# One core, a gated linear attention feeding four experts: the first chunk loaded in rows of four tokens, with new plans for the transfers of the later chunks

## The chip, the cores and the metric

The kernel runs on one core of a Trainium2 chip. The metric is the device time of the program in microseconds (us), as the median of several executions. Each execution comes with the span of its instructions, the clock that TensorE was granted, and a state, fast or slow. A ratio is the mean time of one kernel's fast runs over that of the other's of the same rounds, so it isn't quite the ratio of the medians quoted.

Engines: PE is TensorE, PEld its weight load, DVE VectorE, ACT ScalarE, POOL GpSimd, SP SyncE. SPq and ACTq are the queues on which SyncE and ScalarE issue transfers.

## The reference

```python
B, H, S, D = 4, 8, 768, 48                     # q, k, v, f_logit
f = 1 / (1 + exp(-f_logit))
for t in range(S):
    state = f[:, :, t, :, None] * state + einsum('bhd,bhe->bhde', k[:, :, t], v[:, :, t])
    y[:, :, t] = einsum('bhd,bhde->bhe', q[:, :, t], state)
x = y as (3072, 384)
p = domain_probs / (domain_probs.sum(-1) + 1e-9)
out = sum over 4 experts of p[:, e] * (relu(x @ w1[e]) @ w2[e])     # w1 384x1024, w2 1024x384
```

## The kernel before

The sequence is cut into six chunks of 128 tokens. For each chunk and batch the kernel forms decays (two "gates", a cumulative sum on TensorE, exponentials), multiplies q and k by them, transposes both, multiplies them with each other ("at"), masks the product, multiplies it by v ("y"), and transposes the result into xT, the experts' input. Chunks 0 and 1 are transposed on TensorE, chunks 2 to 5 by a transfer (`dma_tp`).

All instructions are put in order before the program runs. A small planner in Python gives each operation a cost, a priority, its inputs and its buffers, walks through time, and writes the engines' instruction streams in the order that comes out. The hardware then runs each stream strictly in this order.

```python
class Plan:
    def run(self):
        ...
        for e in ("PE", "ACT", "DVE", "POOL", "DMA"):
            ...   # first operation, by priority, whose inputs and buffers are ready
            o.engine, o.start, o.end = e, now, now + o.costs[e]
...
rooms = {"ps_m": 4, "ps_t": 4, "f": 4, "q": 4, "k": 4, "v": 4, ...}     # f, q, k, v: half chunks
...
def load(c, nm, b, n):
    ins[c, nm, b] = nc.sync.dma_start(out=tl(nm, c, b // 2)[:, hh(b, n), :],
                                      in_=srcs[nm][c, :, b * H:(b + n) * H, :])
def dma_tp(c, b):
    nc.sync.dma_start_transpose(out=tl("QK", c, b)..., in_=tl("qk", c, b)...)
...
P.add(f"ld {nm}{c}.{b}", {"DMA": 1.05 * n}, ..., lag=2.0)               # n batches in one load
P.add(f"tp {c}.{b}", {"DMA": 1.8}, on(dma_tp), ..., lag=2.2)
P.add(f"at {c}.{b}", {"PE": 0.35}, on(pe_at), s(7), deps=[et])          # needs tp
P.add(f"store {c}.{nt}.{part}", {"DMA": 0.6}, ...)
...
o.pad, t = int((o.start - t) / 0.2), o.end      # filler matmuls up to the first expert matmul
```

## Time and profile before

| | value |
|---|---|
| time | 304.68 us (304.61 to 305.26, 3 runs) |
| span of the profiled run | 302.7 us |
| first expert matmul | 22.74 us |
| from there to the end ("body") | 280.0 us |
| mean granted clock of TensorE | 0.999 |

Two rows of the page's picture of 40 equal slices: the first is TensorE's busy tenths, the second the clock it was granted.

```profile
PE   7899999999999999999999999999999999999995
...
PEclk9999999999999999999999999999999999999999
```

The table by stretches, asked for the body alone, gives its length, then each engine's busy time (PE first), then granted clock, DMA share and GB/s. TensorE is idle for 280.0 - 274.6 = 5.4 us of the body.

```profile
22.74:302.70 279.96, 274.56 (x1913) 156.62 (x1944) 121.55 (x238) 155.65 (x265) 82.09 (x134) 1.00 0.59 114
```

### The profile page before, as it was taken

What the parts mean: (1) busy time and instruction counts of PE and PEld (TensorE: products, weight loads), DVE (VectorE), ACT (ScalarE), POOL (GpSimd) and SP (SyncE); (2) the same over time, 40 slices, a digit from 0 to 9 for tenths busy, and PEclk for the clock granted to TensorE, in tenths of its full rate; (3) what the DMA queues carried; (4) which work ended last, traced back from release to release, by engine and by line L of the source; (5) the groups of instructions that cost most, each with busy time, mean ns of one, the idle gap of its engine ahead of it and who ended that gap; (6) DMA issues with size and microseconds to landing.
All of it is one profiled execution on the core that took longest, in us unless ns stands there. A gap on an engine that the chain in (4) does not pass through costs nothing.

```text
span 302.7 us, 5517 instructions
## 1 busy us (share of the span) xinstructions
PE 293.2 (97%) x2112; PEld 169.4 (56%) x2143; DVE 138.1 (46%) x273; ACT 170.8 (56%) x295; POOL 95.5 (32%) x157
## 2 busy tenths in 40 slices
PE   7899999999999999999999999999999999999995
PEld 5565555567775655455555555555555555555553
DVE  6774013787853764516555344544423443201223
ACT  5767654857865444676356475345566344475440
POOL 4584400409656237423426143522332100000000
PEclk9999999999999999999999999999999999999999
DMA  7999999954994589866997877301322201100003
GB/s 157 203 193 204 207 206 193 228 83 91 217 207 84 111 161 187 189 122 120 182 187 134 216 142 147 56 13 28 100 61 51 48 14 30 67 22 2 0 0 106
DMA packets 137355, 36.10 MB, mean 119 GB/s; under 512 B 128496, under 2 KB 135792, under 8 KB 137328
## 3 DMA queue, kind: packets, MB, share of 16 engines
q1 hardware_dynamic: 131568, 29.45, 49.1%
q0 software_dynamic: 5760, 6.29, 12.4%
q8 instruction: 17, 0.28, 0.4%
q14 instruction: 10, 0.08, 0.1%
HBM read 31.51 MB, written 4.72 MB: 120 GB/s over the span
## 4 chain that ended last, share of the span: by engine, by line
PE 88%; DMA 4%; DVE 2%; SPq 2%; issue 1%; POOL 1%; ACT 1%; DVEq 0%; ACTq 0%; POOLq 0%
PE ps_m L356 41%; PE ps_m L344 40%; DMA w_sb<-in_moe_w_dram 3%; PE ps_t L300 2%; SPq L222 2%; DMA f<-in_f_logit_dram 1%; PE ps_t L315 1%; PE ps_t L321 1%; PE ps_t L311 1%; PE ps_t L255 1%; PE ps_t L285 1%; DVE qk L276 1%; POOL qk L276 0%; DVE AT L304 0%; POOL Sf L335 0%
## 5 line engine op out<-in xcount | busy, mean ns | idle before, releaser
L352 ACT ACTIVATE h<-ps_m 128x512 bf16<-128x512 f32 (+1 forms) x171 | 98.3, 577 | 103.0 <-PE ps_m L344 92.9
L356 PE MATMUL ps_m<-w_sb,h 128*128 128x384 bf16 x776 | 153.0, 324 | 0.2
L344 PE MATMUL ps_m<-xT,w_sb 128*128 128x512 bf16 (+1 forms) x593 | 150.4, 362 | 2.1 <-DVE o L367 0.3
L356 PEld LDWEIGHTS <-h 128*128 128x128 bf16 x776 | 73.0, 98 | 57.0
L363 DVE SCALAR_TENSOR_TENSOR o<-ps_m,pn,o 128x384 f32<-128x384 f32 (+1 forms) x73 | 44.6, 611 | 96.8 <-PE ps_m L356 89.4
L344 PEld LDWEIGHTS <-w_sb 128*128 128x128 bf16 x624 | 59.8, 98 | 47.1 <-issue 0.7
L276 POOL TENSOR_TENSOR qk<-q,e 128x384 bf16<-128x384 f32 x19 | 22.8, 1204 | 64.9 <-ACT e L262 64.4
L304 DVE TENSOR_TENSOR AT<-ps_t,mask 128x512 bf16<-128x512 f32 x48 | 31.1, 683 | 19.2 <-PE ps_t L300 19.1
L335 POOL TENSOR_TENSOR Sf<-Sf,egs 48x192 f32<-48x192 f32 x40 | 20.4, 510 | 48.8 <-DVE Sf L328 46.8
L350 DVE TENSOR_SCALAR h<-ps_m 128x512 bf16<-128x512 f32 (+1 forms) x37 | 20.7, 572 | 22.0 <-PE ps_m L344 19.8
L276 POOL TENSOR_TENSOR qk<-k,e 128x384 bf16<-128x384 f32 x20 | 21.0, 1052 | 19.8 <-ACT e L264 12.9
L262 ACT ACTIVATE e<-ps_t 128x384 f32<-128x384 f32 x24 | 20.7, 864 | 3.7 <-PE ps_t L255 2.4
L328 DVE TENSOR_TENSOR Sf<-Sf,ps_t 48x192 f32<-48x192 f32 x40 | 14.0, 349 | 6.1 <-PE ps_t L321 5.3
L336 POOL CAST sb<-Sf 48x192 bf16<-48x192 f32 x40 | 13.6, 339 | 2.6
L365 ACT ACTIVATE o<-ps_m,pn 128x384 f32<-128x384 f32 x20 | 11.6, 580 | 3.9 <-PE ps_m L356 3.1
L264 ACT ACTIVATE e<-ps_t 128x384 f32<-128x384 f32 x24 | 13.0, 541 | 0.0
L556 PE MATMUL ps_m<-busy 128*128 128x256 bf16 x71 | 11.5, 301 | 1.3 <-DVE busy L140 1.3
L218 DVE CAST yb<-ps_t 128x384 bf16<-128x384 f32 x16 | 8.9, 555 | 7.4 <-PE ps_t L315 6.3
L247 ACT ACTIVATE ex<-f 128x768 f32<-128x768 f32 (+1 forms) x14 | 10.5, 748 | 3.1 <-DMA f<-in_f_logit_dram 2.9
L315 PE MATMUL ps_t<-vb,AT 128*128 128x48 bf16 x192 | 11.4, 184 | 0.7 <-DVE vb L218 0.7
L315 PEld LDWEIGHTS <-AT 128*128 128x128 bf16 x192 | 9.8, 97 | 3.0 <-issue 1.0
L251 ACT ACTIVATE gp<-ex 128x768 bf16<-128x768 f32 (+1 forms) x14 | 10.5, 751 | 0.4
(50 smaller groups left out, 139.9 us busy)
## 6 DMA issues: line engine op xcount, KB each, us to landing
w_sb<-in_moe_w_dram POOLq DMA_DIRECT2D x8, 768.0 KB, 18.8
out_dram<-o SPq DMA_DIRECT2D x23, 192.0 KB, 2.1
f<-in_f_logit_dram SPq DMA_DIRECT2D x10, 384.0 KB, 4.3
k<-in_k_dram SPq DMA_DIRECT2D x10, 384.0 KB, 5.2
q<-in_q_dram SPq DMA_DIRECT2D x10, 384.0 KB, 5.3
v<-in_v_dram SPq DMA_DIRECT2D x10, 384.0 KB, 5.5
f<-in_f_logit_dram SPq DMA_DIRECT2D x4, 192.0 KB, 4.0
k<-in_k_dram SPq DMA_DIRECT2D x4, 192.0 KB, 4.0
```

The lines of the kernel that those rows point to most:

```text
L262: nc.scalar.activation(out=e[:, 0].rearrange("t (d h) -> t h d", d=D), in_=cs[:, 0:HD].rearrange("t (i r d) -> t r i d", r=2, d=D), func=A ...
L276: engines[eng].tensor_tensor(out=tl("qk", c, b)[:, j, :, 0:D].rearrange("t (i r) d -> t i r d", r=2), in0=tl("qk"[j], c, b // 2)[:, hh(b), ...
L304: nc.vector.tensor_tensor(out=tl("AT", c, b)[:, r].rearrange("s i t -> s (i t)"), in0=tl("A", c, b, r).rearrange("s i t -> s (i t)"), in1= ...
L315: nc.tensor.matmul(out=y[:, h * D:(h + 1) * D], lhsT=AT[:, r, i, :], rhs=vb[:, h, :], start=(c == 0), stop=True, skip_group_check=True)
L328: nc.vector.tensor_tensor(out=Sf[rows, b], in0=Sf[rows, b], in1=KV[rows, :, r, :], op=ALU.add)
L335: nc.gpsimd.tensor_tensor(out=Sf[rows, b], in0=Sf[rows, b], in1=eg, op=ALU.mult)
L336: nc.gpsimd.tensor_copy(out=nb[rows, b, :, r * D:(r + 1) * D], in_=Sf[rows, b])
L344: nc.tensor.matmul(out=tl("hp", c, e, fc, n0)[:, n0:n1], lhsT=w1_sb[:, e, kk, fc * 128:(fc + 1) * 128], rhs=tl("xT", c)[:, kk, n0:n1], sta ...
L350: nc.vector.tensor_relu(out=dst, in_=src)
L352: nc.scalar.activation(out=dst, in_=src, func=AF.Relu)
L356: nc.tensor.matmul(out=tl("op", c, e, nt, part)[:, cols], lhsT=tl("h", c, e)[:, fc, nt * T:(nt + 1) * T], rhs=w2_sb[:, e, fc, cols], start ...
L363: nc.vector.scalar_tensor_tensor(out=o, in0=op, scalar=pe, in1=o, op0=ALU.mult, op1=ALU.add)
```

## The change

The intent is an earlier start of the experts. The first chunk's tokens are dealt out so that a partition row holds four of them. f, q and k then come in packets of 768 B in place of 192 B. Gates and exponentials run over half of the heads for all batches at once; the price is a re-layout of k by 16 small transfers, a permuted mask, and 16 stores for the chunk in place of 4. One PSUM tile holds all eight banks. Alongside, the planning of the later chunks is redone: new costs of transfers, a model of the queue's run-ahead, buffers for whole chunks, exponentials in two planned steps.

```diff
-    LATENCY = 0.2
+    LATENCY, AHEAD = 0.2, 0.06
...
+    def by_tail(self, ops, shift):            # first chunk: priority by the longest way to its end
...
+                    if o.ring is not None:
+                        self.ring = max(self.ring, o.end) + o.ring
+                        o.end = max(o.end, self.ring - 4.0)
+                        o.lag = self.ring - o.end + 1.6
...
-    rooms = {..., "f": 4, "q": 4, "k": 4, "v": 4, ...
+    rooms = {..., "ps_c": 2, "ps_a": 4, "f": 2, "q": 2, "k": 2, "v": 2, ...
+    big = ps.tile([128, 8, 512], FP32, name="big")
...
+    def load0(nm, x, n):
+        if nm == "v":                          # block x: 32 partitions, 192 B runs
+            src = v.rearrange("b h (c p j) d -> c j p (b h) d", p=R, j=J)[0, x]
+            d = nc.sync.dma_start(out=tl("v", 0)[x * R:(x + 1) * R], in_=src)
+        else:                                  # 768 B runs of four tokens
+            src = a.rearrange("b h (c p j) d -> c b p h (j d)", p=R, j=J)[0, b, :, rows]
+            eng = nc.scalar if b % 2 and nm in "fk" else nc.sync
...
-            after(ins["w", 0], ins[0, "k", B - 1])
+            after(ins["w", 0], ins[0, "v", 0])
...
-        op = P.add(f"ld {nm}{c}.{b}", {"DMA": 1.05 * n}, ..., lag=2.0)
+        op = P.add(f"ld {nm}{c}.{b}", {"DMA": 0.6}, ..., ring=1.0 * n)
-        wd[i] = P.add(f"w {i}", {"DMA": 4.5}, ..., lag=2.0)
+        wd[i] = P.add(f"w {i}", {"W": 4.5}, ..., lag=1.5)
-                et = P.add(f"tp {c}.{b}", {"DMA": 1.8}, on(dma_tp), ..., lag=2.2)
+                et = P.add(f"tp {c}.{b}", {"DMA": 1.25}, on(dma_tp), ..., lag=2.9)
-                P.add(f"store {c}.{nt}.{part}", {"DMA": 0.6}, ...)
+                P.add(f"store {c}.{nt}.{part}", {"DMA": 0.45}, ..., ring=0.6)
...
+            for j in range(J):                 # store of the first chunk: four per tile
+                nc.sync.dma_start(out=rows[j], in_=tl("o", c, nt)[j * R:(j + 1) * R, :])
```

## The prediction

> **What bounds the kernel now.** I read the page first, and in it the shares of the engines:
>
> ```profile
> span 302.7 us, 5517 instructions
> PE 293.2 (97%) x2112; PEld 169.4 (56%) x2143; DVE 138.1 (46%) x273; ACT 170.8 (56%) x295; POOL 95.5 (32%) x157
> ```
>
> TensorE is busy for 97% of the span, but 11.5 us of this are 71 filler matmuls on the tile "busy", which only keep it occupied at the start. So two questions decide: when does its real work begin, and does it ever stop afterwards? The waits of TensorE from 23 us to the end answer the second. The columns are total us, times, longest:
>
> ```profile
> PE ps_m L344 <- DVE o L367: 0.3, 1, 0.3
> PE ps_t L285 <- DVE qk L276: 0.3, 1, 0.3
> PE ps_m L344 <- DMA w_sb<-in_moe_w_dram: 0.3, 1, 0.3
> ```
>
> That is the whole list: 0.9 us in 280 us. From the first expert matmul on the kernel is bound by TensorE; nothing that the other engines gain there counts. The timeline of the first 32 us gives that matmul and what ended just before it (start, us, engine, line, operation):
>
> ```profile
> 3.72 0.52 ACT L247 ACTIVATE ex<-f 128x384 f32<-128x384 f32 x1 [1.64 <-DMA f<-in_f_logit_dram]
> ...
> 10.20 1.28 DVE L304 TENSOR_TENSOR AT<-ps_t,mask 128x512 bf16<-128x512 f32 x2
> ...
> 14.63 6.77 POOL L229 DMA_DIRECT2D w_sb<-in_moe_w_dram  x8 [0.25 <-DMA k<-in_k_dram]
> ...
> 18.66 1.87 DVE L304 TENSOR_TENSOR AT<-ps_t,mask 128x512 bf16<-128x512 f32 x3
> ...
> 21.96 0.48 ACT L216 COPY xT<-ps_t 128x384 bf16<-128x384 bf16 x1 [0.73 <-PE ps_t L340]
> 22.74 0.98 PEld L344 LDWEIGHTS <-w_sb 128*128 128x128 bf16 x6 [0.55 <-DMA w_sb<-in_moe_w_dram]
> ```
>
> The first expert matmul starts at 22.74 us. Its input xT is complete at 21.96 + 0.48 = 22.44, its weights at about 22.7. **Two chains end within 0.3 us of each other**, and the change has to shorten both. The chain of waits, cut to 0 to 24 us, names the weights:
>
> ```profile
> 13.03 1.36 POOL qk L276
> 14.38 0.25 issue
> 14.63 8.07 DMA w_sb<-in_moe_w_dram
> ```
>
> The first weight request goes out at 14.63, once the last k has landed, and takes 8.07 us. The other chain is the first chunk's attention. Between 8.70 and 21.60 us the table by stretches has VectorE busy for 11.80 of 12.90 us (ScalarE 9.88): VectorE bounds it.
>
> **What the Trainium skill says.** "DMA: Bandwidth & Descriptors", section Specifications, puts the smallest transfer at line rate at 512 bytes. The trace agrees in direction: 128,496 of the 137,355 packets are under 512 B. In the trace's list of packets the median one of 192 B took 15 ns and one of 768 B 36 ns on its DMA engine; times 16 engines this is 205 and 341 GB/s. "ScalarE: Activation LUTs", What ACT_TABLE_LOAD costs, gives 186 ns + 0.833 ns per column with immediates, hence 506 for 384 columns and 826 for 768; the trace has 523 and 838. One pass of 768 thus saves about 0.2 us against two of 384. "SBUF — State Buffer", Who interferes with whom, says that a VectorE operation with two SBUF inputs blocks against a GpSimd one that reads SBUF. The trace agrees: GpSimd's k product takes 1.36 us in the start while VectorE multiplies, and VectorE's k product takes 0.54 alone there but 0.87 in the mean. So sharing products between them gains less than their count suggests.
>
> **The change, part by part.** Everything named here concerns the first chunk.
>
> *Loads.* f, q and k of the chunk are 3 x 0.786 = 2.36 MB. At 205 GB/s this is 11.5 us, at 341 GB/s 6.9: saved 4.6 us. v stays at 192 B (3.8 us). Traffic begins near 2.4 us, so k should be in SBUF at about 2.4 + 2 x 2.3 + 1 for completion = 8.0, q at 10.3, the first v at 2.4 + 6.9 + 1.0 + 1 = 11.3 and the last v at 14.2 (before: v was used up to 19.0).
>
> *First weights.* Their request now waits for the first v (11.3) in place of the last k (about 14.4). With the measured 8.07 us they arrive at 19.4, 3.3 us earlier. That is a floor for the start. The later ones arrived every 3.9 us of DMA (0.786 MB written at some 205 GB/s); TensorE uses two per 10.3 us (64 units of 0.65 us per chunk, 8 per weight), so no later weight should stop it.
>
> *ScalarE.* Before, four batches had 0.52 + 0.52 + 0.86 + 0.54 + 0.17 = 2.61 us each, 10.4 in all. Now 8 passes of 768 columns at 0.84: 6.7 us. It saves 3.7, but the first products move back: all four batches go through together. f's first half lands near 4.3; two gates to 5.9; two decay sums of 7 matmuls with 1536 columns (0.64 us each at the 0.216 us that 512 columns take) with waits to 7.5; the four exps to about 8.3, 9.0, 9.8 and 10.6. The first product starts at 8.4 instead of 6.42.
>
> *VectorE.* The eight masked copies stay at 0.67 us, 5.4 in all: still PSUM fp32, whatever the mask's type. The q product loses its strided e and should fall from 0.85 to about 0.55, like k's. I assume five of eight products on VectorE at 0.6 (3.0 us), three or four of the eight transposed copies at 0.38 (1.3), and few v and y copies, since ScalarE is free from 10.6. Sum 9.7 us, against 12.65 between 6.4 and 21.6 before. From 8.4, with 1 us lost waiting for q and for the first masked copy: 19.1.
>
> *The end of the chain.* From the last masked copy (18.66 + 1.87 = 20.53) to xT (22.44) were 1.9 us: y, its copy, transposes, their copy. The same four steps remain. 19.1 + 1.9 = 21.0; if more goes to ScalarE and GpSimd than I assume, 19.5. I take **20.5** as the start, against 22.74: 2.2 us.
>
> *Moved off the path.* The k tile is laid out again by 16 small transfers and the state sums wait for them; at some 0.5 us an issue they end near 24 us, and TensorE needs the last at about 26. Single PSUM tile, fewer pads, split exps of later chunks, other orders there: TensorE's work after the start is the same, so 0 us. The first chunk's stores become 4 issues each, near 80 us, where SyncE has slack.
>
> **Rivals.** *Weights bind alone:* if the attention is quicker than I think, the start stops at 19.4 (a gain of 3.3; 301.4 us). For it: the request still waits for 6.9 us of loads. *The attention is hardly quicker:* gathering all batches in one tile loses the overlap that batch 0 had (its first masked copy was at 10.20; now about 12.5). With VectorE then packed to 20 us the start is 22 and the time 304. For it: VectorE was the bound and its masked copies stay. *A new stall in TensorE's order:* state sums waiting for the k transfers behind the weight traffic, or the second chunk coming late because its requests are planned behind all weights; up to 2 us lost, 304 to 306. Against it: its first load still waits for the sixth weight, which itself comes earlier. *A wider gain,* over 6.1 us (2%), would need a start by 16.6, before the weights can be there: nearly excluded.
>
> **Range and chances.** 304.68 - 2.2 = 302.5; I lean slightly to the smaller side of the time, since the planner's priorities were redone for just this stretch: 302.3. Lower end 300.2: start at 18.3, weights a microsecond earlier than worked out. Upper end 304.5: the gain all but eaten by one of the two losing rivals. Both 2% lines (298.6 and 310.8) lie outside.
>
> **What would show it.** Right: packets of 192 B fewer by some 12,000; k used before 9 us; first weight request near 11.3; first masked copy near 12.5; the first expert matmul between 19.4 and 21.5; the difference of the times equal to the difference of these starts within 0.5 us; VectorE over 85% busy from 9 us to the last masked copy. Wrong: TensorE waits over 0.5 us after its start (third rival); the first expert matmul waiting for weights by over 1 us (first rival); or VectorE idle in the start, waiting for ScalarE or loads, which my sum does not contain.

## More of the kernel before

SyncE's queue near 70 to 93 us (start, us taken, line, operation, tensors, how many) shows the loads of chunk 2, the stores of chunk 0 and the first transposing transfers of chunk 2 sharing one queue:

```profile
71.23 0.59 SPq L222 DMA_DIRECT2D f<-in_f_logit_dram  x1
71.92 1.59 SPq L222 DMA_DIRECT2D k<-in_k_dram  x1
...
81.64 1.76 SPq L371 DMA_DIRECT2D out_dram<-o  x1
...
88.92 1.34 SPq L289 DMA_TRANSPOSE QK<-qk  x1
...
92.25 2.13 SPq L289 DMA_TRANSPOSE QK<-qk  x1
```

## The result and the profile after

| | before | after |
|---|---|---|
| time, median | 304.97 us (304.61 to 305.79, 4 runs) | 333.39 us (332.97 to 333.98, 4 runs) |
| span of the profiled run | 302.7 | 332.3 |
| first expert matmul | 22.74 | 27.47 |
| body | 280.0 | 304.8 |
| mean granted clock | 0.999 | 0.952 |

The ratio is 1.093 (1.090 to 1.096). The kernel became 28 us slower, far outside the range. Of the 29.6 us between the spans, **4.7 are a later start and 24.8 are in the body**, where the prediction had put zero.

The page's two rows show the body's loss. Three holes in TensorE's row (slices 12, 14 and 19 of 40) each stand beside a fall of the clock; a fourth fall, in slice 10, has no hole above it:

```profile
PE   5989999989959599995999999999999999999995
...
PEclk9959999995978989997899999999999999999999
```

The table by stretches, for the body of the changed kernel:

```profile
27.47:332.30 304.83, 287.30 (x1946) 160.96 (x1943) 122.13 (x239) 156.84 (x269) 80.37 (x132) 0.96 0.59 104
```

TensorE is idle for 304.8 - 287.3 = 17.5 us, 12.1 more than before. Its busy time grew by 12.7 us, although it does the same work after the start. The trace's clock records give four stretches of half clock in the body, 23.9 us in all, in which matmuls take about twice as long. TensorE was busy for 21.1 us of them; half of that, some 10.6 us, is most of the growth. The kernel before has none between 5.4 us and its last microsecond.

The list of TensorE's waits after the start (us in total, times, longest) names what it stood for. Like the body, it is read from one profiled execution of each kernel:

```profile
PE big L455 <- DMA QK<-qk: 7.8, 3, 3.8
PE big L413 <- ACT gp L329: 4.1, 2, 3.8
PE big L465 <- DVE AT L459: 0.5, 1, 0.5
```

L455 is "at", which waits for the transposed q and k (3.6 of the 7.8 us fall in chunk 2, the rest in chunk 3), and L413 the cumulative sum, which waits for the gates and so for f. SyncE's queue shows what is behind both:

```profile
69.80 8.55 SPq L530 DMA_DIRECT2D out_dram<-o  x16
...
80.27 0.51 SPq L283 DMA_DIRECT2D f<-in_f_logit_dram  x1
...
99.49 1.35 SPq L444 DMA_TRANSPOSE QK<-qk  x1
...
102.22 1.25 SPq L444 DMA_TRANSPOSE QK<-qk  x1
...
110.87 2.89 SPq L444 DMA_TRANSPOSE QK<-qk  x1
```

The 16 stores hold the queue for 8.55 us, f of chunk 2 is issued at 80.27 in place of 71.23, and the transposes at 99 to 115 in place of 89 to 105. It is tempting to stop here and blame the stores. The first experiment shows why that is not the cause.

The start, on ScalarE (start, us, what its idle time was waiting for):

```profile
5.94 0.84 ACT L332 ACTIVATE ex<-f 128x768 f32<-128x768 f32 x1 [3.85 <-DMA f<-in_f_logit_dram]
...
10.46 1.51 ACT L348 ACTIVATE e<-big 128x768 f32<-128x768 f32 x2 [1.12 <-PE big L344]
13.23 1.51 ACT L348 ACTIVATE e<-big 128x768 f32<-128x768 f32 x2 [1.26 <-PE big L344]
18.48 0.51 ACT L277 CAST vb<-v 128x384 bf16<-128x384 f32 x1 [3.73 <-DMA v<-in_v_dram]
18.90 1.55 ACT L277 COPY QK<-big 112x512 bf16<-112x512 bf16 x3
```

f arrives late, the decay sums take twice the predicted time (1.28 us; in s_warm below, with TensorE kept busy ahead of them, 0.66), and then ScalarE stands for v with three ready copies of q and k behind it.

### The profile page after: what moved, and what is told of

Read it like the earlier page. It is cut to its first block, busy times and chain, and to the rows that moved or that the text cites. A ratio compares the mean times of both kernels' runs of the same rounds, so it can differ in the third digit from the quotient of the medians.

```text
span 332.3 us, 5660 instructions
## 1 busy us (share of the span) xinstructions
PE 308.5 (93%) x2137; PEld 176.1 (53%) x2137; DVE 136.9 (41%) x268; ACT 170.6 (51%) x291; POOL 99.2 (30%) x165
## 4 chain that ended last, share of the span: by engine, by line
PE 74%; DMA 13%; issue 3%; SPq 3%; DVE 2%; ACT 2%; POOL 1%; ACTq 0%; POOLq 0%; DVEq 0%
PE big L510 34%; PE big L498 33%; DMA QK<-qk 4%; DMA f<-in_f_logit_dram 3%; DMA qk<-h 3%; PE big L455 2%; DMA v<-in_v_dram 2%; SPq L409 1%; SPq L283 1%; PE big L341 1%; DMA xT<-yb 1%; PE big L413 1%; PE big L469 1%; PE big L465 1%; PE big L475 1%
## 5 line engine op out<-in xcount | busy, mean ns | idle before, releaser
L498 PE MATMUL big<-xT,w_sb 128*128 128x512 bf16 (+1 forms) x624 | 158.6, 372 | 0.0
L506 ACT ACTIVATE h<-big 128x512 bf16<-128x512 f32 (+1 forms) x167 | 96.0, 578 | 117.5 <-PE big L498 107.9
L510 PE MATMUL big<-w_sb,h 128*128 128x384 bf16 x776 | 156.3, 329 | 0.0
L517 DVE SCALAR_TENSOR_TENSOR o<-big,pn,o 128x384 f32<-128x384 f32 (+1 forms) x73 | 44.6, 612 | 104.0 <-PE big L510 86.1
L504 DVE TENSOR_SCALAR h<-big 128x512 bf16<-128x512 f32 (+1 forms) x41 | 23.5, 580 | 33.4 <-PE big L498 33.1
L459 DVE TENSOR_TENSOR AT<-big,mask 128x512 bf16<-128x512 f32 x40 | 25.9, 685 | 22.7 <-PE big L455 22.6
L418 ACT ACTIVATE e<-big 128x384 f32<-128x384 f32 x20 | 17.3, 865 | 2.1 <-PE big L413 2.0
L482 DVE TENSOR_TENSOR Sf<-Sf,big 48x192 f32<-48x192 f32 x40 | 14.0, 350 | 9.5 <-PE big L475 8.7
L519 ACT ACTIVATE o<-big,pn 128x384 f32<-128x384 f32 x23 | 13.3, 580 | 5.4 <-PE big L510 4.7
L455 PE MATMUL big<-QK 48*128 48x128 bf16 x160 | 8.4, 227 | 8.0 <-DMA QK<-qk 7.8
L455 PEld LDWEIGHTS <-QK 48*128 48x128 bf16 x160 | 4.7, 97 | 15.4 <-DMA QK<-qk 9.7
L421 ACT ACTIVATE e<-big 128x384 f32<-128x384 f32 x20 | 10.9, 543 | 0.0
L465 PE MATMUL big<-sb,QK 112*128 112x96 bf16 x80 | 10.2, 206 | 0.6 <-DVE AT L459 0.5
L469 PE MATMUL big<-vb,AT 128*128 128x48 bf16 x160 | 10.4, 187 | 0.4 <-DVE AT L459 0.4
```

The lines of the kernel that those rows point to most:

```text
L418: nc.scalar.activation(out=e[:, 0].rearrange("t (d h) -> t h d", d=D), in_=cs[:, 0:HD].rearrange("t (i r d) -> t r i d", r=2, d=D), func=A ...
L455: nc.tensor.matmul(out=tl("A", c, b, r)[:, i, :], lhsT=QK[rows, 1, i, :], rhs=QK[rows, 0, i, :], start=True, stop=True)
L459: nc.vector.tensor_tensor(out=tl("AT", c, b)[:, r].rearrange("s i t -> s (i t)"), in0=tl("A", c, b, r).rearrange("s i t -> s (i t)"), in1= ...
L469: nc.tensor.matmul(out=y[:, h * D:(h + 1) * D], lhsT=AT[:, r, i, :], rhs=vb[:, h, :], start=False, stop=True, skip_group_check=True)
L482: nc.vector.tensor_tensor(out=Sf[rows, b], in0=Sf[rows, b], in1=KV[rows, :, r, :], op=ALU.add)
L498: nc.tensor.matmul(out=tl("hp", c, e, fc, n0)[:, n0:n1], lhsT=w1_sb[:, e, kk, fc * 128:(fc + 1) * 128], rhs=tl("xT", c)[:, kk, n0:n1], sta ...
```

## The experiments

Eighteen kernels ran. All gave correct results unless said otherwise. "QK wait" is TensorE's total wait for transposed q and k after the start, "start" the first expert matmul, "body" span minus start; these three come from one profiled execution each. The two main theories are these. One: the first chunk's own traffic (its stores, its many issues, its late start) delays the later chunks. The other, called C from the third round on: the new planning of the later chunks puts steps that wait for transfers too early in TensorE's fixed order. The kernel before ran in the same rounds; its medians there were 304.57 to 304.89 us, but 309.96 where several of its runs were slow.

### First round: undoing single suspects in the changed kernel

**m_move**: the 16 stores go behind chunk 2's loads (with ten output buffers in place of six).

```diff
+    late = [o for o in done if o.name.startswith("store 0.")]      # moved behind "ld v2.2"
-"o": 6
+"o": 10
```

> The 16 store issues of the first chunk (8.6 us of SyncE at 69.8 to 78.5 us) are moved behind the second chunk-after-next's loads; nothing else of the order changes (6 more KB of output buffers make room). Theory 'stores block the queue': the f load of chunk 2 goes out near 71.5 instead of 80.3, its gate runs near 86 instead of 95, the TensorE gap of 3.8 us at 90 to 97 and the half-speed clock that follows it go, 322 us or less. Rival 'everything is simply late and the loads stand ahead of the transposes in the queue': the gaps at 110 and 150 us stay and the time is 328 to 333.

Measured: 338.67 us, ratio 1.112; start 26.5, body 309.5. f of chunk 2 went out at 76.65 instead of 80.27. But the stores then stood ahead of the transposes, which came at 103.7, and the QK wait rose to 16.8 us. The blockade moved and cost more. "Only the stores" falls.

**m_late**: the plan is told that the first chunk ends 7.4 us later.

```diff
+        for kk in range(KD):
+            xdone[0, kk].lag += 7.4
```

> The planner is told that the first expert matmul starts at 27.4 us, as measured, instead of 20.0; no instruction is added or removed, only the orders after the start change (the stores then fall among the loads of chunk 2, the transposes of chunk 2 stay behind loads of chunk 3). Theory 'plan and chip drifted apart': TensorE waits after 30 us fall from 14 us to under 5, time 312 or less. Rival 'queue order of loads and transposes as such': over 322.

Measured: 334.06 us, ratio 1.097; start 32.1, body 300.0, QK wait 12.2. My text was wrong in one thing: the planner fills the gap it now sees with some 37 filler matmuls, and these pushed the real start to 32.1 us. The body was 4.8 us shorter, but the edit is confounded: the expected 312 us was missed, and the time over 322 is the one that the text's rival, the order of SyncE's queue as such, had named.

**s_warm** and **s_dve** go for the start: 20 more filler matmuls ahead of the first decay sum, and all first-chunk products on VectorE.

```diff
+            if o.name == "cs 0.0":
+                o.pad += 20
```

> 20 more filler matmuls before the first decay sum, so that TensorE does not idle from 5.3 to 7.7 us. Theory 'TensorE lost its full clock to that gap': the decay sums take 0.64 us each instead of 1.28, the second pair of exps starts near 11 instead of 13.2, first expert matmul near 25 instead of 27.5. Rival 'products and loads set the start': first expert matmul stays within 0.6 us of 27.5.

```diff
-km = P.add(f"k 0.{i}", {"DVE": 0.65, "POOL": 1.1}, ...      # and the same for q
+km = P.add(f"k 0.{i}", {"DVE": 0.65}, ...
```

> All eight products of the first chunk on VectorE, none on GpSimd. Theory 'they block each other': VectorE's products take 0.56 us each instead of 0.56 to 1.68, the eight need some 4.5 us as the four did before, the first weight request no longer waits behind a GpSimd product (from 16.3 to under 15), first expert matmul near 26.5. Rival 'GpSimd carries half the work': the first masked copy moves back by 1.5 us or more, start 28.5 or later.

Measured: 335.0 us (start 28.1) and 334.65 us (start 29.9). Both did their own step: in s_warm the exponentials ran back to back from 9.19 to 12.3 us, in s_dve the products took 0.50 to 0.56 us. Neither moved the start forward. ScalarE's timeline of s_warm says why:

```profile
9.19 3.12 ACT L348 ACTIVATE e<-big 128x768 f32<-128x768 f32 x4
18.68 0.51 ACT L277 CAST vb<-v 128x384 bf16<-128x384 f32 x1 [6.38 <-DMA v<-in_v_dram]
19.10 1.55 ACT L277 COPY QK<-big 112x512 bf16<-112x512 bf16 x3
```

The 2.4 us saved ahead of it became 2.65 us more of waiting for v (6.38 instead of 3.73).

### Second round: parts of the change alone

**b1**: the first chunk of the kernel before inside all the rest of the change (new planning, whole-chunk buffers, split exponentials, one PSUM tile). The edit restores the old loads, decay sums, exponentials and stores of chunk 0.

> The first chunk as in the kernel before (192-byte rows, batch by batch, one store per tile), all planning of the later chunks, the whole-chunk buffers, the split exps and the one PSUM tile as in the changed kernel; its plan puts the first expert matmul at 30.4 us, later than the chip reached it before (22.7). Theory A 'the plan runs ahead of the chip because of the first chunk (late start, 16 stores counted as 4)': start near 22.7, no waits of TensorE over 2 us in all after it, 304 to 308 us. Theory B 'the new transfer costs and orders of the later chunks are themselves at fault': waits for the transposes stay, 315 us or more.

Measured: 329.96 us, ratio 1.082; start 34.9, body 292.0, QK wait 10.1. The new first chunk isn't needed for the QK waits. But b1's body is only 12.0 us above that of the kernel before: the other 12.8 of the 24.8 us appear only with the new first chunk in place. The start of 34.9 us was a surprise, and is taken up below.

**m_true**: the plan is told the start (27.4 us, the fillers ahead of it held at 3), the stores' 2.2 us each, and a landing of 6.0 us for the transposes.

```diff
+            xdone[0, kk].lag += 7.4                     # and o.pad = 3 for "h 0."
-"store ...", {"DMA": 0.45}
+"store ...", {"DMA": 0.45 if c else 2.2}
-"tp ...", lag=2.9
+"tp ...", lag=6.0
```

> The changed kernel with three numbers of its plan set to what the trace shows: first expert matmul at 27.4 us (fillers before it held at 3), a first-chunk store 2.2 us of the queue instead of 0.45, landing of a transposed transfer 6.0 us after its issue instead of 2.9. Same instructions, other orders. Theory A: TensorE's waits for transposes fall from 7.8 us to under 2, start 27.5, time 310 to 315. Theory B: falls too, but by less than half. If the waits stay as they are, the queue itself and not the plan is what limits.

Measured: 328.09 us, ratio 1.076; start 26.9, body 298.3. The waits for QK came in under 2 us as expected, the time missed its 310 to 315. The QK wait fell from 7.8 to 0.7 us, but 4.3 us for a late ReLU and 4.2 us for xT of chunk 2 took its place. Telling the plan one truth moves the wait to the next untruth.

**m_one** (wrong: one store per tile, so the first chunk's rows of the output are permuted) and **s_v** (the plan told that a load of v takes 1.9 us):

```diff
-        if c:
+        if True:
             nc.sync.dma_start(out=out[r0:r0 + T, cols], in_=tl("o", c, nt)[:, cols])
```

> WRONG RESULT ON PURPOSE: the first chunk's tiles are stored by one transfer each (rows in the wrong order), so that 12 of the 16 issues go; plan and order are those of the changed kernel. If the issues themselves cost: f of chunk 2 goes out near 74 to 76 instead of 80.3 and the time falls by 5 us or more. If the queue waits for the exps of chunk 1 anyway (as with the stores moved): by less than 3 us.

```diff
+    for x in range(B):
+        ld[0, "v", x].ring = 1.9
```

> The planner is told that a first-chunk v takes 1.9 us of the ring, not 1.0, so that ScalarE's v casts come later in its order. Theory 'ScalarE stands at the v cast (3.7 us from 14.8 to 18.5) with the transposed copies behind it': that wait goes, the second pair of masked copies starts near 18 instead of 20.3, first expert matmul at 25.5 or earlier. Rival 'loads of q and v bound it directly': start within 0.7 us of 27.5. The later stalls stay.

Measured: m_one 331.64 us (body 302.2, QK wait 11.7), so without the twelve extra stores the body is only 2.6 us shorter. s_v 333.79 us with a start of 28.7: the casts of v moved behind the copies on ScalarE, but one went to VectorE, which then held its masked copies back until 18.67 us.

### Third round: the kernel before with one part added

These start from the other side, with nothing of the change but one part. **d_mem** takes the memory (one PSUM tile, whole-chunk buffers); its plan is that of the kernel before, step for step. **d_plan** takes the planning of the later chunks' transfers, **d_exps** the split exponentials of chunks 1 to 5. **e_old2** is the complement: the changed kernel with the old costs for the later transfers.

> The kernel before, in its own planned order to the instruction (the plan is the same line by line), with only the memory of the change: one PSUM tile for all eight banks and input buffers for a whole chunk instead of half a chunk. Theory C (the body's 24.8 us are lost because the new planning puts chunk 2's attention too early in TensorE's fixed order: 62.5 us of expert work stand ahead of the first product of chunk 2 that needs the transposed q and k, where the kernel before has 72.8 us): no loss here, 303 to 307 us, hardly any wait of TensorE after the start. Rival M (one PSUM tile or the larger buffers make false dependences or slower loads): 312 us or more.

> The kernel before, its first chunk and its buffers untouched, with only the change's planning of the later chunks' transfers (loads at 0.6 us with a run-ahead of 4 us, weights on a resource of their own, new costs of stores and transposes, choice 0.06 us ahead). The plan then puts 65.0 us of expert work ahead of chunk 2's first product, where the kernel before has 72.8 us. Theory C: the start stays near 22.7 us, but TensorE waits 4 to 12 us for the transposed q and k of chunk 2, its clock falls to half after each wait, and the time is 311 to 325 us. Rival (planning is harmless, the loss needs the new first chunk): 303 to 307 us.

> The kernel before with only the exponentials of chunks 1 to 5 split into two planned steps. 71.5 us of expert work stand ahead of chunk 2's first product (kernel before 72.8). Theory C: 303 to 308 us. Rival (the split exponentials make the loss): over 312 us.

> The changed kernel with its new first chunk, its buffers and its PSUM tile, but the later chunks' transfers planned with the costs of the kernel before (first-chunk stores at their measured 2.2 us each). 75.3 us of expert work stand ahead of chunk 2's first product. Theory C: the start stays at 27 to 29 us, the waits for transposed q and k nearly vanish, half clock disappears around 80 to 120 us, the body falls from 304.8 to 280 to 290 us, and the time to 308 to 318 us. Rival (the body's loss comes from the new first chunk's late start, its 16 stores or its buffers): 325 us or more.

| | time | start | body | QK wait |
|---|---|---|---|---|
| d_mem | 313.45 (311.18 to 315.72) | 33.2 | 280.7 | 0 |
| d_plan | 325.3 fast, 334.7 slow | 34.5 | 298.4 (slow run) | 10.3 |
| d_exps | 308.07 (306.43 to 309.72) | 24.5 | 280.1 | 0 |
| e_old2 | 324.78 (324.40 to 325.17) | 28.4 | 294.3 | 0 |

Memory and split exponentials leave the body at 280 to 281 us: these two suspects are out as single parts. d_exps ended just outside its 303 to 308, by its start of 24.5. d_mem's time missed its 303 to 307 for another reason, its start. e_old2 missed its 308 to 318: it has no QK wait left, but a new one of 8.1 us for the re-laid k. My own edit had sent early loads of the probabilities ahead of that re-layout. d_plan's profile fell in a slow run, so it proves nothing alone.

The late starts of b1, d_mem and d_plan have one form. In d_mem TensorE waited 10.2 us for a cast that waited for v. The trace's list of packets shows it: from 20 to 25 us some 90 packets of 192 B per microsecond were moved beside some 90 weight packets of 2048 B; at 14 to 16 us it had been some 1,025 per microsecond. The Trainium skill, "DMA: Bandwidth & Descriptors", Queues, rings and completion order, says that each DMA engine takes turns between its queues packet by packet. The one-to-one counts agree with that (a packet of the page can hold several of the trace's, and the trace shows only the counts): once the weights flow, each small packet is paid for with a large one of 172 ns, and 90 of these fill 15.5 of the 16 engines' microseconds. Whether v's last packets get through before the first weights is a close race: the first weight request went out 0.3 us before SyncE's last issue of v ended in the kernel before, and 1.5, 1.4 and 0.6 us before it in d_mem, d_plan and b1.

### Fourth round: planning alone, cleanly

**b_hold** takes the race away: the kernel before, in its own order, with the first weight request held until the last v has landed. For this the weight requests also move behind the last load of v in the order (not shown below). **d_ph** is b_hold with the change's planning of the later transfers, and nothing else: the new costs, the model of the queue's run-ahead, the weights off the plan's queue, other dependences of the loads, and a look-ahead of 0.06 us.

```diff
-            after(ins["w", 0], ins[0, "k", B - 1])
+            after(ins["w", 0], ins[0, "v", B - 1])
```

> The kernel before in its own order, with one thing changed: the first weight request waits until the last load of v has landed, not the last load of k. If the late starts of 33 us in three runs came from the weights overtaking the tail of v: no run over 309 us, v landed by 19 us, first expert matmul at 23.5 to 25.5 us because the weights come later, time 305.5 to 308 us, body 280 us. If not: some runs with starts over 30 us.

> The same as b_hold, with the change's planning of the later chunks' transfers in addition; the first chunk is that of the kernel before. Theory C: start 23.5 to 26 us as in b_hold, but waits for transposed q and k of 5 to 12 us with half clock after them, body 290 to 300 us, time 315 to 326 us. Rival (planning alone is harmless, d_plan only suffered from its late start): body 280 to 284 us, time within 4 us of b_hold.

Measured: b_hold 310.12 us (309.16 to 311.50, 4 runs), start 26.6, no late start, but 4.2 us of waiting for the weights and half clock after it, so more than expected. d_ph 327.81 us (327.45 to 328.92, 4 runs), ratio 1.076, start 26.2. The starts agree within 0.4 us, so the two differ in their bodies. Stretches of b_hold, then of d_ph:

```profile
26.57:309.20 282.63, 278.79 (x1944) 157.45 (x1944) 121.05 (x234) 155.78 (x265) 82.25 (x134) 0.99 0.58 113
```

```profile
26.19:326.20 300.01, 283.20 (x1944) 158.44 (x1944) 118.97 (x228) 157.97 (x271) 82.42 (x134) 0.98 0.55 107
```

**The planning alone costs 17.4 us of body**, 13.0 of them as idle time. And now compare the queues. The transposes of chunk 2 in b_hold:

```profile
95.58 1.33 SPq L289 DMA_TRANSPOSE QK<-qk  x1
98.90 1.62 SPq L289 DMA_TRANSPOSE QK<-qk  x1
...
109.04 2.93 SPq L289 DMA_TRANSPOSE QK<-qk  x2
```

The same in d_ph, and TensorE's wait for them:

```profile
94.41 1.34 SPq L295 DMA_TRANSPOSE QK<-qk  x1
97.19 1.25 SPq L295 DMA_TRANSPOSE QK<-qk  x1
105.97 2.35 SPq L295 DMA_TRANSPOSE QK<-qk  x1
...
109.72 1.25 SPq L295 DMA_TRANSPOSE QK<-qk  x1
```

```profile
PE ps_t L306 <- DMA QK<-qk: 11.5, 5, 3.8
```

In d_ph all four transposes of chunk 2 are *earlier*, yet TensorE waits for them, and in b_hold not at all. Of the 11.5 us 4.3 fall in chunk 2, the rest in chunk 3. How much work TensorE's order holds in front of a product can be counted in expert matmuls since the start (by their weight loads, of which the traces miss none). Here are the five products that waited in d_ph:

| chunk.batch | matmuls ahead, b_hold / d_ph | its transpose issued, b_hold / d_ph | wait in d_ph, us |
|---|---|---|---|
| 2.0 | 390 / 346 | 95.6 / 94.4 | 0.8 |
| 2.2 | 436 / 387 | 109.0 / 106.0 | 3.5 |
| 3.0 | 555 / 530 | 133.4 / 138.5 | 1.9 |
| 3.2 | 600 / 600 | 142.2 / 156.3 | 1.5 |
| 3.3 | 635 / 635 | 151.2 / 166.8 | 3.8 |

In chunk 2 the difference is TensorE's order: fewer matmuls ahead, and the transfers not later. In the last two of chunk 3 that order is the same, and the transfers are later, by SyncE's order: in d_ph they left 5.5 and 6.7 us after their inputs were ready (0.6 and 0.0 in b_hold), because loads for chunks 4 and 5 stood ahead of them. **The new plan moves products forward on TensorE and puts later loads ahead of transposes on SyncE**. It thought it could afford both: it counts on a load of two batches taking 0.6 us of the queue (until its model is 4 us behind), while the eight loads of chunk 2 took 1.22 us each in the kernel before (9.78 us together).

**e_p**: the changed kernel with the old transfer costs, and the probabilities left where the change has them. **e_pl**: e_p, with the plan told the true start of 27.4 us.

```diff
-{"DMA": 0.6} ..., ring=1.0 * n            # ld
+{"DMA": 1.05 * n} ..., lag=2.0
-{"DMA": 1.25} ..., lag=2.9                # tp; likewise xt, egs, store (2.2 us in chunk 0)
+{"DMA": 1.8} ..., lag=2.2
+            xdone[0, kk].lag += 7.4       # e_pl only, with o.pad = 3 for "h 0."
```

> The changed kernel with the first chunk, buffers, PSUM tile and split exponentials of the change, and the later chunks' transfers planned with the costs of the kernel before; unlike e_old2 the loads of the domain probabilities keep the change's place, so nothing stands ahead of the re-layout of k. Theory C (planning of the later chunks makes the body's loss): start 27 to 29 us, no wait for the re-laid k, body 281 to 287 us, time 309 to 316 us. Rival (the first chunk's 16 stores, 40 early issues or late start make the body's loss): body over 292 us, time over 320 us.

> e_p with the plan told that the first expert matmul comes at 27.4 us (the fillers ahead of it held at 3, so that they don't push it). If the optimistic start is what is left of the body's loss: body 281 to 285 us, half clock after 30 us at most once, time 309 to 314 us. Rival (the 16 first-chunk stores or the split exponentials cost it): body 287 us or more, time 316 us or more.

Measured: e_p 318.16 us (315.84 to 318.48, 4 runs), ratio 1.042, start 27.7, body 288.6: 16.2 us of body came back, though body and time both stayed 1.6 to 2.2 us above my range. e_pl 311.72 us (310.80 to 312.25, 4 runs), ratio 1.024, start 27.1, body 282.0. TensorE's waits after the start in e_pl are two:

```profile
PE big L510 <- DVE h L504: 2.1, 1, 2.1
PE big L475 <- DMA qk<-h: 0.3, 1, 0.3
```

All 16 stores, the late start, the whole-chunk buffers and the split exponentials are still in e_pl. With the plan put right they cost 2.0 us of body together. In e_p the transposes of chunk 2 went out at 99.7, 105.3, 112.8 and 118.1 us, all four later than in the changed kernel, and no product waited for them: 408 expert matmuls stood in front. What was left in e_p is a wait of 2.5 us for xT and two stretches of half clock of 3.4 us each.

The plan's figures in this table, and those of the plan below, are the planner's own, printed while the kernel is built. They are beliefs, not times.

| | plan: TensorE's work from the start through chunk 2's first product, us | expert matmuls ahead of it in the trace | QK wait, us | body, us |
|---|---|---|---|---|
| before | 72.8 | 390 | 0 | 280.0 |
| after | 62.5 | 326 | 7.8 (3.6 in chunk 2) | 304.8 |
| d_ph | 65.0 | 346 | 11.5 (4.3 in chunk 2) | 300.0 |
| e_p | 76.0 | 408 | 0 | 288.6 |
| e_pl | 70.8 | 380 | 0 | 282.0 |

Where the texts call the first column "expert work", it is this: TensorE's other planned work in that stretch is some 9 us of it. In the changed kernel the first product of chunk 2 itself did not wait; the third did, for 3.6 us, with 369 matmuls ahead of it against 436 in b_hold.

### The start

**x_vw** (wrong: v of the first chunk in plain token order, one transfer per batch over 128 partitions, so its rows don't match; with s_warm's fillers).

```diff
-            src = v.rearrange("b h (c p j) d -> c j p (b h) d", p=R, j=J)[0, x]
-            d = nc.sync.dma_start(out=tl("v", 0)[x * R:(x + 1) * R], in_=src)
+            src = v.rearrange("b h (c t) d -> c t b h d", t=T)[0, :, x]
+            d = nc.sync.dma_start(out=tl("v", 0)[:, x * H:(x + 1) * H, :], in_=src)
```

> Wrong on purpose. The changed kernel with 20 more filler matmuls ahead of the first decay sum (as in s_warm, which started at 28.1 us) and v of the first chunk loaded in plain token order, 128 partitions to a transfer as in the kernel before, so its rows do not match. If v's 32-partition layout makes it land late and ScalarE's wait for it sets the start: v landed by 15.5 us, ScalarE's wait of 6.4 us shrinks below 3 us, start 24 to 26 us. Rival (the start is set by something else after the exponentials): start stays at 27 us or later.

Measured: start 25.9 us against 28.1 of s_warm, time 333.12 us. ScalarE's wait for v shrank from 6.38 to 1.42 us:

```profile
9.45 3.12 ACT L348 ACTIVATE e<-big 128x768 f32<-128x768 f32 x4
13.99 0.51 ACT L277 CAST vb<-v 128x384 bf16<-128x384 f32 x1 [1.42 <-DMA v<-in_v_dram]
17.17 0.59 ACT L277 COPY QK<-big 112x512 bf16<-112x512 bf16 x1 [2.66 <-PE big L373]
```

So v's layout costs 2.2 us of the start. Two things differ with it, and this run doesn't part them. Packets of v took 15 ns in each microsecond's median, against 26 to 33 ns in s_warm. And the first cast, which takes one batch on all 128 partitions, needs only the first transfer here, but all four 32-partition blocks in the changed layout. That the body was still 305 us shows once more that the start isn't the main loss.

**e_vo** tries a correct remedy: e_pl with s_warm's fillers, and the four blocks of v issued in the order 0, 2, 1, 3. The Trainium skill, "SBUF — State Buffer", Door 1: The DMA port swizzle, says that partitions 0 to 31 reach only half of the ports and that 32 to 63 share these.

```diff
-[(nm, x, 8) for nm in "kqv" for x in range(B)]
+[(nm, x, 8) for nm in "kq" for x in range(B)] + [("v", x, 8) for x in (0, 2, 1, 3)]
```

> e_pl with two changes of the start: 20 more filler matmuls ahead of the first decay sum (as in s_warm, which alone gained nothing) and v's four transfers of 32 partitions issued in the order of blocks 0, 2, 1, 3 in place of 0, 1, 2, 3. If neighbouring blocks (partitions 0 to 31 and 32 to 63) share their ports and blocks 0 and 2 do not: v's packets take under 22 ns, v lands by 17 us, the start is 25 to 26.5 us in place of 27.1, time 309 to 311 us. Rival (a 32-partition transfer is slow by itself): packets stay at 26 to 31 ns, start 26.5 us or later, time 311 to 313 us.

Measured: 312.64 us median, ratio 1.024 (1.021 to 1.027), the same as e_pl. The profile fell in a slow run. In it packets of v took 16 to 22 ns in place of s_warm's 26 to 33, but the first cast still came at 18.04 us. In e_pl, with the old order, they took 15 to 31 ns, so that the order matters even for the packets is not shown. It doesn't mend the start. How much of the 2.2 us is the packets' slowness, and how much the wait for all four blocks, stays open.

No version of the changed kernel beat the kernel before. The nearest was e_pl, 2.4% slower.

## Why the prediction was wrong

**The bound was read rightly, and that was the trap.** TensorE is the bound from the first expert matmul on. In the before profile it waits 0.9 us in 280. The prediction turned this into "TensorE's work after the start is the same, so 0 us" for single PSUM tile, fewer pads, split exps and "other orders there". This is the step that failed, with 24.8 us. The work is the same, but its order is not, nor is the order of the transfers on SyncE's queue. A wait list that is nearly empty says that the present order leaves enough work in front of each wait. It doesn't say that any order does. The diff showed the new costs in plain sight, and the prediction, which says "Everything named here concerns the first chunk", never priced them.

What the runs showed in its place: the new planning of the later transfers alone makes 17.4 us of body (d_ph against b_hold), by products moved forward on TensorE and by loads put ahead of transposes on SyncE. Which part of it does most, no run isolates. Taking the new costs out of the changed kernel returns 16.2 (e_p), correcting the plan's start returns 6.6 more (e_pl against e_p), and 2.0 remain. Memory and split exponentials, for which "0 us" was right, cost under 1 us (d_mem, d_exps).

**The clock doubles the price.** The third rival had the right form, "A new stall in TensorE's order", but named the state sums or the second chunk and put it at "up to 2 us"; the waits came in the third and fourth chunks (2 and 3). Its sign, "TensorE waits over 0.5 us after its start", came true: it was 12.1 us of idle time, and 12.7 us of added busy time, some 10.6 of it from the half clock, that the prediction had no term for. The Trainium skill, "TensorE: Matmul & The Clock Gate", Part 1, tells that TensorE falls to half rate after about 3.4 us of idleness and needs as long to return. The traces agree in the steps: half clock lasted a whole number of times 3.41 us in every run (the stretch cut off by a trace's end aside). In the idleness they don't quite agree; the last section has the figures. The prediction left the clock out; the clock row of the kernel before, all nines, gave no hint of it.

**The stores.** "near 80 us, where SyncE has slack" failed: they held the queue for 8.55 us. But by m_one and e_pl this is a small part, not the cause.

**The start** was to be 20.5 us and was 27.47:

| term | predicted | after | what the runs say |
|---|---|---|---|
| f's first half in SBUF | 4.3 | 5.94 | eight issues of 0.75 and 0.86 us in the mean, on two queues |
| two decay sums | 0.64 us each | 1.28 us each | half clock; s_warm mends it |
| four exponentials done | 10.6 | 14.74 | follows from the two above; 12.3 in s_warm |
| first product | 8.4 | 11.33 | the same |
| last v | 14.2 | 18.4 | its layout (x_vw), not the compute |
| last masked copy | 19.1 | 25.48 | ScalarE's copies behind v |
| first weight request | 11.3 | 16.34 | behind a GpSimd product; weights not binding |

The one term that an experiment isolates is v, 2.2 us: the prediction gave v its old 3.8 us and did not see that its new layout, four blocks of 32 partitions, delays the first cast. With that and the half rate out of the way (x_vw) the start was 25.9, still 5.4 us above the predicted 20.5; no run parts these 5.4 us further. A later masked copy was listed as a rival ("The attention is hardly quicker") with a start of 22 us. The direction was right, the size was not. f, q and k did come in packets of 768 B, which took 36 ns as predicted (the prediction had read this from the last stores; other 768 B packets of the kernel before, on GpSimd's queue, took 79). The loads reached 326 to 333 GB/s, but only from 9 to 11 us; from 3 to 9 us they ran at 177 to 301 GB/s.

## What to carry to other kernels

When instructions run in a fixed order, an empty wait list is a property of that order, so a diff that touches the planner's costs needs a price for every wait it could open: how much work stands in front of it now and in the new order, and what stands ahead of the transfer in its own queue. A plan that is too pessimistic costs little (the one before expected its start at 25.05 us and its chunk-2 transposes at 95.0, the chip gave 22.74 and 88.92), while one that is too optimistic (20.01 and 84.0, against 27.47 and 99.49) stops the bound engine. And on TensorE add the half clock to a wait of several microseconds: waits of 3.5 to 3.8 us (changed kernel, d_ph) were followed by 3.4 or 6.8 us at half clock, so by 1.7 to 3.4 us more if TensorE is busy; one of 2.1 us (e_pl) was followed by none.

## What the Trainium skill lacked or had wrong

- "TensorE: Matmul & The Clock Gate", Part 1, and Why this matters for your kernels speak of an idle window, or gaps, of some 3 us and more. Here partly busy windows were enough. In e_p the window of 3.41 us before a fall at 78.3 us had TensorE busy for 2.38 us, with no wait over 0.4 us; in the changed kernel the windows before its four falls in the body had 2.19, 0.88, 0.32 and 0.78 us. The matmuls of the first case are the small ones of the attention. That a wait can also pass without a fall is in e_pl: 2.1 us up to 82.8 us, and no half clock. The section A second HAM failure mode does name frequent short idle times as a cause; what the page lacks is how busy a window may be and still lose the clock.
- "DMA: Bandwidth & Descriptors", Specifications, gives a smallest size for line rate. Its section Issuing engines are not separate DMA queues calls the time to issue usually small beside the transfer. Here it was not: 768 B packets took the expected 36 ns, but f's eight transfers of 98 KB needed 3.01 and 3.45 us to issue on two queues, and loads ran at 177 to 301 GB/s until 9 us. The compiled program uses eight completion semaphores in rotation for these queues, and four early issues start within 0.02 us of a landing on the same semaphore; that this sets the pace is a reading, no run isolates it.
- "SBUF — State Buffer", Door 1, tells that 32 partitions reach half the ports. It gives rates but no packet times: 192 B packets took 15 ns into 128 partitions (x_vw) and 26 to 33 ns into 32-partition blocks one after the other (s_warm), though 15 to 31 ns in e_pl with the same order, and 16 to 22 ns with the order changed (e_vo, a slow run).
- "DMA: Bandwidth & Descriptors", Queues, rings and completion order, describes the turns between queues. What it lacks is the consequence for a small transfer under a large one: v's tail fell from some 1,025 to about 90 packets a microsecond, and the last cast of v came at 28.8 us in d_mem in place of 19.0.
